# A causal convolution followed by a gated feed-forward layer: third channel group of the first chunk in bf16 on VectorE, a new order of the first loads, and a reordered VectorE list in the first step

## The chip, the cores and the metric

The kernel runs on one core of a Trainium2 chip. The metric is the device time of one execution in microseconds (us), the median of several; lower is better. TensorE is called PE below, its weight loads PEld, VectorE DVE, ScalarE ACT, GpSimd POOL, and SyncE, which issues most loads and stores, SP. A small letter q (SPq, ACTq) marks an engine's sequencer, for example when it issues a transfer.

An execution that takes over 1.5% more than the fastest of the same kernel is called slow here, the others fast. One of the kernel before took 1214.12 us and is left out.

## The reference

```python
# attention-like part: a causal convolution with one softmaxed 7-tap filter per head
w = softmax(weight, axis=-1)                 # (8 heads, 7 taps)
out[b, s, h, g] = sum_k w[h, k] * x_pad[b, s + k, h, g]    # x is (8, 4096, 192), group 24
# feed-forward part on (32768, 192)
h = x @ w_in                                 # 192 -> 2048
g = h * sigmoid(beta * h)                    # beta per feature
y = g @ w_out                                # 2048 -> 192, fp32 out
```

## The kernel before

The tokens are worked in 32 steps. A step takes 512 tokens of two sequences. The 192 channels of a token lie as three groups (c = 0, 1, 2) of 64; the two sequences fill 128 partitions. In a step PE makes 16 blocks of 128 features ("hidden"); ACT applies Silu to each block, and PE multiplies finished blocks with w_out ("output pairs"). The convolution for step s + 2 runs on DVE during step s.

Some names: a tap is one of the seven multiply-adds of the filter; cw holds the softmaxed filter weights; x0, x1 and xf are the loaded tokens of chunks 0, 1 and 2, and x0b, x1b and xb their bf16 copies; ct is the finished convolution; ph is a block of hidden features in PSUM, the memory into which PE writes, and g the block after Silu; pa and pb are PSUM tiles, of output pairs and, early in step 0, of other work. A load "lands" when its transfer is complete.

Step 0 is special, because nothing is ready for it. Its convolution is split: groups 0 and 1 on PE (products with diagonal matrices), group 2 with five taps on DVE and two on PE. Chunk 1 (the tokens of step 1) is prepared inside step 0 as well, its group 0 on PE and its groups 1 and 2 on DVE.

```python
    load_x(x0, 0)                                  # SP's queue, in this order
    nc.sync.dma_start(out=beta_q, in_=...)
    ...                                            # w_in_raw: first 256 columns, fp32, two transfers
    load_x(x1, TOK)                                # chunk 1
    for i in range(NW - 1):
        load_w_out(i)
    load(2)                                        # chunk 2
    ...
    hold = setup.tile([1, 1], BF16)                # POOL issues the other w_in columns, cast to bf16,
    nc.gpsimd.tensor_copy(hold, x0b[0:1, 0, 0, 0, 0:1])   # once the first x0 rows are cast
    load_w_in(F0, FW)
    for i in range(1, NW):
        load_w_in(i * FW, (i + 1) * FW)
    ...
    nc.scalar.copy(w_in_s[:, :, 0:F0], w_in_raw)   # ACT's list: first columns, then x1 casts and ct
    new_ct(0)
    for c in range(NG - 1):                        # groups 0 and 1: seven taps on PE
        ...
        for b in ((0, 1), (2,))[c]:
            cast_rows(nc.scalar.copy, x1b, x1, b)
        nc.scalar.copy(cts[0][:, c, :], pv[:, 0, :])
    cast_rows(nc.scalar.copy, x1b, x1, NB - 1)
    ...
    K_V = 5                                        # group 2: taps 5, 6 on PE, taps 0..4 on DVE
    pv = in_a()[:, 0, :]
    for k in range(K_V, K):
        diag_tap(k, xt0[:, NG - 1], pv, k0=K_V)
    dst = cts[0][:, NG - 1, :]
    for k in range(K_V):
        o = HALO - PAD + k
        tap(dst, xt0[:, NG - 1, o : o + TOK].bitcast(FP32), k)
    nc.vector.tensor_tensor(dst, pv, dst, ALU.add)
    ...
    first_work = {                                 # DVE's list in step 0, by block; None = next tap of chunk 1
        4: [None, lambda: scale_w_out(1), None],
        5: [None],
        6: [conv1_evac, lambda: scale_w_out(2), lambda: rows_of(2), None],
        8: [None, lambda: scale_w_out(3)],
        9: [None],
        10: [None],
    }
    QUOTA_A = {4: 2, 7: 5}                         # output pairs PE does in early blocks of step 0
```

`rows_of(2)` casts chunk 2 and starts its transposes; `scale_w_out(i)` divides a quarter of w_out by beta and casts it.

Of the kernel before, what the change touches and what calls it, by code (L numbers as in the profile page):

```python
# [9 lines left out]
FP32 = mybir.dt.float32  # L10
FP32R = mybir.dt.float32r
# [6 lines left out]
def kernel(  # L18
# [62 lines left out]
    def in_a():  # L81
        return psum_a.tile([128, 2, TOK], FP32, name="pa")
# [67 lines left out]
    w8 = setup.tile([H, K], FP32)  # L150
    nc.scalar.dma_start(out=w8, in_=weight)
    beta_q = setup.tile([NF, 128], FP32)


    def load_x(dst, t0):
        for i in range(2):
            t = t0 + i * 2 * BLK
            nc.sync.dma_start(  # L158
                out=dst[:, i].rearrange("q h b d -> q h (b d)"),
                in_=x_v[0, t : t + 2 * BLK, :, :].rearrange(  # L160
                    "(q b) h d -> q h (b d)", b=2
                ),
            )

    load_x(x0, 0)
    nc.sync.dma_start(out=beta_q, in_=moe_beta.rearrange("(c p) -> c p", p=128))
    F0 = 256
    w_in_raw = setup.tile([128, NG, F0], FP32)
    for r in range(2):
        nc.sync.dma_start(  # L170
            out=w_in_raw[r * DG : (r + 1) * DG], in_=w_in_v[:, :, 0:F0]
        )
    load_x(x1, TOK)
    for i in range(NW - 1):
        load_w_out(i)
    load(2)
# [5 lines left out]
    warm = setup.tile([H, 1], FP32)  # L182
    nc.vector.memset(warm, 0.0)  # L183
    nc.scalar.activation(warm, warm, AF.Exp)  # L184
    xt0 = setup.tile([128, NG, HALO + TOK], FP32R)
    nc.vector.memset(xt0[:, :, 0:HALO].bitcast(FP32), 0.0)

    sel = setup.tile([H, 2, DG], FP32)
    nc.gpsimd.memset(sel, 1.0)
# [38 lines left out]
    def cast_rows(copy, xb, x, b):  # L228
        copy(  # L229
            xb[:, b].rearrange("q c h p -> q h c p"),  # L230
            x[:, b // 2, :, b % 2].rearrange("q h (p c) -> q h c p", c=NG),
        )

    def transposes(pt, xb, b):
        for c in range(NG):
            nc.tensor.transpose(
                pt[:, c, :], xb[:, b, c].rearrange("q h p -> q (h p)"), ident_b
            )

    def tokens(xt, b):  # L240
        t = HALO + (b // 2) * 2 * BLK
        return xt[:, :, t : t + 2 * BLK].rearrange("p c (q b) -> p c b q", b=2)[:, :, b % 2]


    fill(3)
    pw = in_a()[:, 0, 0:K]
    nc.tensor.matmul(pw, sel.rearrange("i h p -> i (h p)"), w8, start=True, stop=True)
    fill(5)
    nmax = setup.tile([128, 1], FP32)
# [12 lines left out]
    def diags(k0, k1):  # L262
        nc.vector.tensor_tensor(
            diag[:, k0:k1],
            ident.unsqueeze(1).to_broadcast((128, k1 - k0, 128)),
            cw[:, k0:k1].unsqueeze(2).to_broadcast((128, k1 - k0, 128)),
            ALU.mult,
        )

    for b in range(NB):  # L270
        cast_rows(nc.vector.tensor_copy, x0b, x0, b)
        if b == 1:
            diags(0, 2)
    diags(2, 4)
    diags(4, K)


    hold = setup.tile([1, 1], BF16)
    nc.gpsimd.tensor_copy(hold, x0b[0:1, 0, 0, 0, 0:1])
    load_w_in(F0, FW)  # L280
    for i in range(1, NW):
        load_w_in(i * FW, (i + 1) * FW)
# [4 lines left out]
    def new_ct(s):  # L287
        cts[s] = ct_pool.tile([128, NG, TOK], BF16, name="ct")

    def diag_tap(k, xt, pv, rows=slice(0, 128), k0=0):  # L290
        o = HALO - PAD + k
        nc.tensor.matmul(  # L292
            pv,
            diag[rows, k, :],
            xt[rows, o : o + TOK],
            start=(k == k0),
            stop=(k == K - 1),
        )

# [1 line left out]
        pool.tile([128, 2, 2 * TOK], BF16, name=name)  # L301
        for pool, name in ((psum_b, "pb"), (psum_h, "ph"))
    ]
    for b in range(NB):
        pt = pts[b % 2][:, b // 2, 0 : NG * BLK].rearrange("p (c q) -> p c q", c=NG)
        transposes(pt, x0b, b)
        nc.scalar.copy(tokens(xt0, b), pt)  # L307
        if b % 2:
            fill(1, 384)
    pb = in_a()[:, 0, 0:NF]  # L310
    nc.tensor.transpose(pb, beta_q, ident[0:NF, 0:NF])
    nc.scalar.copy(beta, pb)
    fill(1, 256)
    nc.scalar.copy(w_in_s[:, :, 0:F0], w_in_raw)

    def scale_w_out(i):
        fcs = slice(i * NQ, (i + 1) * NQ)
# [9 lines left out]
    for c in range(NG - 1):  # L327
        pv = in_b() if c else psum_h.tile([128, 2, TOK], FP32, name="ph")
        for k in range(K):
            diag_tap(k, xt0[:, c], pv[:, 0, :])  # L330
        for b in ((0, 1), (2,))[c]:
            cast_rows(nc.scalar.copy, x1b, x1, b)
        nc.scalar.copy(cts[0][:, c, :], pv[:, 0, :])
    cast_rows(nc.scalar.copy, x1b, x1, NB - 1)

    def tap(dst, src, k):
        scalar = cw[:, k : k + 1]
# [4 lines left out]
                out=dst, in0=src, scalar=scalar, in1=dst, op0=ALU.mult, op1=ALU.add  # L342
            )

    K_V = 5
    pv = in_a()[:, 0, :]
    for k in range(K_V, K):
        diag_tap(k, xt0[:, NG - 1], pv, k0=K_V)
    dst = cts[0][:, NG - 1, :]
    for k in range(K_V):  # L350
        o = HALO - PAD + k
        tap(dst, xt0[:, NG - 1, o : o + TOK].bitcast(FP32), k)
    nc.vector.tensor_tensor(dst, pv, dst, ALU.add)
    nc.vector.reciprocal(beta_r, beta)
    scale_w_out(0)

# [1 line left out]
    def second():  # L358
        xt = new_xt(1)
        for i in range(2):  # L360
            pt = (in_b, in_a)[i]()
            for b in range(2):
                for c in range(NG):
                    for r in range(2):
                        rows = slice(r * DG, (r + 1) * DG)
                        o = (c * 2 + b) * DG
                        nc.tensor.matmul(
                            pt[:, r, o : o + DG],
                            x1b[rows, 2 * i + b, c].rearrange("q h p -> q (h p)"),
                            ident_b[rows, rows],  # L370
                            start=True,
                            stop=True,
                        )
            t = HALO + i * 2 * BLK
            for r in range(2):
                nc.vector.tensor_copy(
                    xt[:, :, t + r * BLK : t + (r + 1) * BLK].rearrange(
                        "p c (q b) -> p c q b", b=2
                    ),
                    pt[:, r, 0 : NG * BLK].rearrange("p (c b q) -> p c q b", c=NG, b=2),  # L380
                )
        halo(1, xt0)
        nc.vector.tensor_copy(xt1[:, HALO - PAD :], xt[:, 0, HALO - PAD :])


# [53 lines left out]
    class Job:  # L439
# [27 lines left out]
        def leave(self):  # L467
            nb = self.nb
            osb = osb_pool.tile([128, 2, D], FP32, name="osb")
            dst = osb[:, 0:nb, :].rearrange("p b d -> p (b d)")  # L470
            if nb == 1:
                nc.scalar.copy(dst, self.po[:, 0, 0:D])  # L472
            else:
                nc.vector.tensor_reduce(  # L474
                    dst,
                    self.po[:, :, 0 : nb * D].rearrange("p r n -> p n r"),
                    axis=mybir.AxisListType.X,
                    op=ALU.add,
                )
            p, c = divmod(self.s, CHUNKS)  # L480
            t = c * TOK + self.q * BLK
            nc.sync.dma_start(
                out=out_v[self.h, p, t : t + nb * BLK, :].rearrange(
                    "(b q) d -> q b d", q=BLK
                ),
                in_=osb[:, 0:nb, :],
            )
# [33 lines left out]
    def rows_of(ch):  # L521
        for h in range(2):
            cast(ch, h)
        xpose(ch)
# [2 lines left out]
    first_work = {  # L527
        4: [None, lambda: scale_w_out(1), None],
        5: [None],
        6: [conv1_evac, lambda: scale_w_out(2), lambda: rows_of(2), None],  # L530
        8: [None, lambda: scale_w_out(3)],
        9: [None],
        10: [None],
    }

    QUOTA_A = {4: 2, 7: 5}
    queue = deque()
    for s in range(N_ST):
        jobs_of(s)
        for u in range(NF):  # L540
            if s > 0 or u > 1:
                hidden(s, u)
            elif u == 0:
                phs = [hidden(0, fc, [0]) for fc in range(2)]
                for j in range(1, NG):
                    for fc in range(2):
                        hidden(0, fc, [j], phs[fc])
                second()
            if s > 0:
                output(s, u, 8 if s < N_ST - 1 else 7, "ab")  # L550
            elif u > 7:
                output(s, u, 5 if u < NF - 1 else 10, "ab")
            elif u in QUOTA_A:
                output(s, u, QUOTA_A[u], "a")
            if s == 0:
                if u in CONV1:
                    conv1(u)
                if u == min(CONV1):
                    queue.extend(conv_ops(1, 1))
                for work in first_work.get(u, []):  # L560
                    (work or queue.popleft())()
            else:
                if u % 2 and queue:
                    queue.popleft()()

                if u == 0 and s + 3 < N_CH:
                    load(s + 3)
                if u < 2 and s + 2 < N_CH:
                    cast(s + 2, u)
                if u == 1 and s + 2 < N_CH:  # L570
                    xpose(s + 2)
            if u == 12 and s + 2 < N_CH:
                queue.extend(conv_ops(s + 2, 0))
# [32 lines left out]
```

## Time and profile before

| | kernel before |
|---|---|
| first three executions | 690.76 us, 692.39 us, and the one of 1214.12 us that is left out |
| span of the profiled execution | 690.1 us |
| PE busy from 36 to 80 us | 44.00 of 44.00 us |
| first Silu; first Silu of step 1 | 13.21 us; 31.82 us |

The head of the profile page, busy time and share of the span:

```profile
span 690.1 us, 24341 instructions
PE 682.9 (99%) x11312; PEld 521.7 (76%) x11312; DVE 523.2 (76%) x466; ACT 579.8 (84%) x532; POOL 8.2 (1%) x19
```

The table by window, with the columns: stretch, its length, then busy time (and number of instructions) of PE, PEld, DVE, ACT and POOL, the granted PE clock, the DMA share and GB/s:

```profile
28.00:30.00 2.00, 2.00 (x34) 1.82 (x31) 1.97 (x3) 2.00 (x3) 0.00 (x0) 1.00 0.23 40
...
36.00:58.00 22.00, 22.00 (x374) 16.81 (x370) 18.55 (x18) 18.71 (x18) 0.00 (x0) 1.00 0.42 109
```

From 36 to 668 us the windows show no idle time of PE at all, so every microsecond that an edit of step 0 saves or costs must show in when step 1 starts.

ACT's timeline in step 0 of the kernel before. Columns: start, length, engine, line, operation, out<-in, shape, number of instructions merged; in brackets the idle time before and what ended it:

```profile
13.21 4.14 ACT L431 ACTIVATE g<-ph,beta 128x1024 bf16<-128x1024 f32 x4 [0.52 <-PE ph L423]
17.79 1.11 ACT L431 ACTIVATE g<-ph,beta 128x1024 bf16<-128x1024 f32 x1 [0.44 <-PE ph L423]
19.11 2.24 ACT L431 ACTIVATE g<-ph,beta 128x1024 bf16<-128x1024 f32 x2 [0.21 <-PE ph L423]
21.59 9.59 ACT L431 ACTIVATE g<-ph,beta 128x1024 bf16<-128x1024 f32 x9 [0.24 <-PE ph L423]
31.82 1.11 ACT L431 ACTIVATE g<-ph,beta 128x1024 bf16<-128x1024 f32 x1 [0.63 <-PE ph L423]
```

Nine Silus take 9.59 us, about 1.06 us a block. The first four Silus start 1.01 us apart, and there PE waits for ACT (the "<-ACT g" further below). From block 5 on it is PE that sets the pace: it is busy 12.00 of 12.00 us from 18 to 30 us, and each Silu starts about 0.04 us after PE's last product of its block (the ends of products are modelled). One block on PE, from the chain of waits of a second profile of this kernel (before_again; start, length, what), is 1.06 us too:

```profile
25.65 0.65 PE ph L423 x6
26.29 0.16 PE pa L456 x4
26.46 0.25 PE pb L456 x6
```

The gaps of 0.21 and 0.24 us before Silus 5 and 7 (counted from 0) lie in this stretch, in which PE is never idle: beside the blocks it works chunk 1's group 0 there. The gap of 0.44 us at 17.79 follows a wait of PE for a slice of w_in, in PE's timeline:

```profile
16.40 0.37 PE L423 MATMUL ph<-ct,w_in_s 64*128 64x512 bf16 x1 [0.20 <-ACT g L431]
16.93 0.82 PE L423 MATMUL ph<-ct,w_in_s 64*128 64x512 bf16 x5 [0.16 <-DMA w_in_s<-in_moe_w_in_dram]
```

DVE's timeline around group 2 of chunk 0 and around the casts of chunk 2:

```profile
7.86 0.49 DVE L339 TENSOR_SCALAR ct<-xt,cw 128x512 bf16<-128x512 f32 x1 [0.18 <-ACT xt L307]
8.38 3.11 DVE L341 SCALAR_TENSOR_TENSOR ct<-xt,cw,ct 128x512 bf16<-128x512 f32 x4
11.96 0.69 DVE L353 TENSOR_TENSOR ct<-pa,ct 128x512 bf16<-128x512 f32 x1 [0.46 <-PE pa L292]
...
24.46 0.69 DVE L106 CAST xb<-xf 128x768 bf16<-128x768 f32 x1 [0.56 <-DMA xf<-in_x_dram]
...
27.66 0.95 DVE L318 TENSOR_TENSOR w_out_s<-w_out_raw,beta_r 128x768 bf16<-128x768 f32 x1
28.52 2.60 DVE L341 SCALAR_TENSOR_TENSOR ct<-xt,cw,ct 128x1024 bf16<-128x1024 bf16 x2
```

And the chain of waits of this execution (start, length, what) from 8 to 32 us:

```profile
8.61 15.83 DMA xf<-in_x_dram
...
29.84 1.30 DVE ct L341
...
31.18 0.61 PE ph L423 x4
```

The reader sees two chains that end step 0 almost together: the blocks, which PE makes and ACT finishes with a Silu and which start when group 2 is ready ("the Silus" below), and DVE's list, which waits for chunk 2.

### The profile page before, as it was taken

To read this page: it belongs to the slowest core of one execution; us is meant where nothing else is said; L and a number is where in the kernel's file an instruction comes from. 1 tells how busy PE (TensorE), PEld (TensorE's weight loads), DVE (VectorE), ACT (ScalarE), POOL (GpSimd) and SP (SyncE) were. 2 spreads that over 40 slices of the span, in tenths; PEclk is the share of its full clock that TensorE was granted. 3 is DMA by queue.
4 is the path that set the end of the run, shared out by engine and by line. 5 is a ranking of instruction groups with operands and counts; after the bars stand their busy time and mean duration, and the time that the engine had idled before them with its cause. 6 is when DMAs were issued, how large, how long until landed. Compare 5 with 4: busy or idle time off the path is not lost.

```text
span 690.1 us, 24341 instructions
## 1 busy us (share of the span) xinstructions
PE 682.9 (99%) x11312; PEld 521.7 (76%) x11312; DVE 523.2 (76%) x466; ACT 579.8 (84%) x532; POOL 8.2 (1%) x19
## 2 busy tenths in 40 slices
PE   8999999999999999999999999999999999999997
PEld 4877777777777777777777777777777777777776
DVE  6888877788777797777797777887777977777721
ACT  7888888888888888888888888888888888888883
POOL 4000000000000000000000000000000000000000
PEclk9999999999999999999999999999999999999999
DMA  9744332244332343332444332443322443322111
GB/s 234 175 110 116 105 94 77 75 116 116 94 102 65 91 116 107 100 101 56 103 117 105 94 90 62 116 116 96 103 70 83 117 114 89 104 54 59 48 36 59
DMA packets 121861, 67.06 MB, mean 97 GB/s; under 512 B 53264, under 2 KB 121760, under 8 KB 121760
## 3 DMA queue, kind: packets, MB, share of 16 engines
q1 hardware_dynamic: 120080, 64.13, 34.4%
q0 software_dynamic: 1664, 1.38, 1.2%
q8 instruction: 88, 1.44, 0.9%
q14 instruction: 13, 0.11, 0.1%
q10 hardware_dynamic: 16, 0.00, 0.0%
HBM read 29.89 MB, written 25.17 MB: 80 GB/s over the span
## 4 chain that ended last, share of the span: by engine, by line
PE 95%; DMA 3%; DVE 1%; SPq 0%; ACT 0%; issue 0%
PE ph L423 47%; PE pa L456 24%; PE pb L456 24%; DMA xf<-in_x_dram 2%; DVE ct L341 1%; DMA x<-in_x_dram 1%; SPq L95 0%; ACT g L431 0%; SPq L148 0%; DVE w_out_s L318 0%; DVE xb L106 0%; SPq L158 0%; ACT osb L472 0%; DVE xt L121 0%
## 5 line engine op out<-in xcount | busy, mean ns | idle before, releaser
L431 ACT ACTIVATE g<-ph,beta 128x1024 bf16<-128x1024 f32 x512 | 569.6, 1114 | 96.6 <-PE ph L423 90.7
L456 PEld LDWEIGHTS <-g 64*128 64x128 bf16 x8160 | 371.2, 94 | 102.5 <-ACT g L431 0.7
L423 PE MATMUL ph<-ct,w_in_s 64*128 64x512 bf16 x3072 | 425.6, 376 | 1.3 <-ACT g L431 1.1
L341 DVE SCALAR_TENSOR_TENSOR ct<-xt,cw,ct 128x1536 bf16<-128x1536 bf16 (+2 forms) x190 | 337.6, 1777 | 2.5
L456 PE MATMUL pa<-w_out_s,g 64*128 64x192 bf16 x4112 | 246.6, 243 | 0.5 <-ACT g L431 0.5
L456 PE MATMUL pb<-w_out_s,g 64*128 64x192 bf16 (+1 forms) x4048 | 230.9, 243 | 0.0
L423 PEld LDWEIGHTS <-w_in_s 64*128 64x128 bf16 x3072 | 160.2, 94 | 55.4 <-DMA w_in_s<-in_moe_w_in_dram 1.8
L474 DVE TENSOR_REDUCE osb<-pa 128x384 f32<-128x768 f32 x64 | 61.3, 957 | 125.3 <-PE pa L456 125.2
L474 DVE TENSOR_REDUCE osb<-pb 128x384 f32<-128x768 f32 x63 | 60.5, 960 | 26.8 <-PE pb L456 26.8
L106 DVE CAST xb<-xf 128x768 bf16<-128x768 f32 x60 | 41.2, 686 | 0.6 <-DMA xf<-in_x_dram 0.6
L339 DVE TENSOR_SCALAR ct<-xt,cw 128x1536 bf16<-128x1536 bf16 (+2 forms) x32 | 31.2, 974 | 0.2 <-ACT xt L307 0.2
L472 ACT COPY osb<-pb 128x192 f32<-128x192 f32 x1 | 0.3, 318 | 6.5 <-PE pb L456 6.5
L226 PE MATMUL ph<-zeros 128*128 128x512 bf16 (+2 forms) x11 | 4.4, 513 | 1.1 <-DVE warm L183 1.1
L214 POOL DMA_DIRECT2D w_in_s<-in_moe_w_in_dram x8 | 5.1, 647 | 0.0
L292 PE MATMUL pb<-xt,diag 64*128 64x512 f32 (+1 forms) x21 | 5.0, 434 | 0.0
L121 DVE COPY xt<-xt 128x18 bf16<-128x18 bf16 x27 | 4.7, 175 | 0.0
L292 PEld LDWEIGHTS pb<-xt,diag 64*128 64x128 f32 (+1 forms) x21 | 3.1, 187 | 0.7
L318 DVE TENSOR_TENSOR w_out_s<-w_out_raw,beta_r 128x768 bf16<-128x768 f32 x3 | 2.9, 954 | 0.0
L226 PEld LDWEIGHTS <-zeros 128*128 128x128 bf16 x11 | 1.2, 121 | 2.2 <-issue 1.1
L229 ACT CAST x1b<-x 128x384 bf16<-128x384 f32 x4 | 2.7, 708 | 0.0
L184 ACT ACT_TABLE_LOAD x1 | 1.3, 1283 | 1.4 <-PEq L590 1.4
L229 DVE CAST x0b<-x 128x384 bf16<-128x384 f32 x4 | 1.6, 434 | 0.9 <-DMA x<-in_x_dram 0.9
(53 smaller groups left out, 26.3 us busy)
## 6 DMA issues: line engine op xcount, KB each, us to landing
out_dram<-osb SPq DMA_DIRECT2D x127, 192.0 KB, 2.2
xf<-in_x_dram SPq DMA_DIRECT2D x60, 384.0 KB, 4.2
xt<-xb SPq DMA_TRANSPOSE x120, 2.5
x<-in_x_dram SPq DMA_DIRECT2D x4, 384.0 KB, 5.0
w_out_raw<-in_moe_w_out_dram SPq DMA_DIRECT2D x4, 384.0 KB, 12.8
w_in_s<-in_moe_w_in_dram POOLq DMA_DIRECT2D x6, 192.0 KB, 10.7
w_in_raw<-in_moe_w_in_dram SPq DMA_DIRECT2D x2, 192.0 KB, 5.0
w_in_s<-in_moe_w_in_dram POOLq DMA_DIRECT2D x2, 96.0 KB, 7.5
```

The costliest lines, as they stand in the source:

```text
L106: nc.vector.tensor_copy(xbs[ch][:, :, :, h, :], xfs[ch][:, h].rearrange("q b (p c) -> q b c p", c=NG),)
L121: nc.vector.tensor_copy(dst, last[:, :, HALO + TOK - PAD :])
L214: nc.gpsimd.dma_start(out=w_in_s[r * DG : (r + 1) * DG, :, c0:c1], in_=w_in_v[:, :, c0:c1])
L226: nc.tensor.matmul(pf[:, 0, 0:cols], zeros, zc, start=True, stop=True)
L229: copy(xb[:, b].rearrange("q c h p -> q h c p"), x[:, b // 2, :, b % 2].rearrange("q h (p c) -> q h c p", c=NG),)
L292: nc.tensor.matmul(pv, diag[rows, k, :], xt[rows, o : o + TOK], start=(k == k0), stop=(k == K - 1),)
L339: nc.vector.tensor_scalar_mul(dst, src, scalar)
L341: nc.vector.scalar_tensor_tensor(out=dst, in0=src, scalar=scalar, in1=dst, op0=ALU.mult, op1=ALU.add)
L423: nc.tensor.matmul(ph[:, h, :], w_in_s[rows, j, fc * 128 : (fc + 1) * 128], cts[s][rows, j, :], start=(j == 0), stop=(j == NG - 1),)
L431: nc.scalar.activation(gs[s][:, fc], ph, AF.Silu, scale=beta[:, fc : fc + 1])
L456: nc.tensor.matmul(self.po[:, r, b * D : (b + 1) * D], g[rows, fc, self.h, q * BLK : (q + 1) * BLK], w_out_s[rows, fc, :], start=(self.don ...
L474: nc.vector.tensor_reduce(dst, self.po[:, :, 0 : nb * D].rearrange("p r n -> p n r"), axis=mybir.AxisListType.X, op=ALU.add,)
```

## The change

Its intent: let DVE read group 2 as bf16 and finish it without PE; bring chunk 1 in before the first w_in columns; release the other w_in slices as soon as cw exists; and put DVE's list in the order in which the loads land, so that two taps come ahead of the wait for chunk 2. ACT's list changes with it: the cast of the first w_in columns moves behind the first copy of ct. Cut to its core:

```diff
+    nc.scalar.dma_start(out=beta_q, in_=...)              # was on SP's queue, after x0
     load_x(x0, 0)
+    load_x(x1, TOK)                                       # was after w_in_raw
...
-    nc.gpsimd.tensor_copy(hold, x0b[0:1, 0, 0, 0, 0:1])
+    nc.gpsimd.tensor_copy(hold, cw[0:1, 0:1])
...                                                        # third transposes go to pt_v, DVE copies them out
+        nc.vector.tensor_copy(
+            xt0_v[:, t : t + 2 * BLK].rearrange("p (q b) -> p b q", b=2), pt_v[:, i]
+        )
...
-    nc.scalar.copy(w_in_s[:, :, 0:F0], w_in_raw)
...
+        if c == 0:
+            for b in range(2):
+                cast_rows(nc.scalar.copy, x1b, x1, b)
         nc.scalar.copy(cts[0][:, c, :], pv[:, 0, :])
+        if c == 0:
+            nc.scalar.copy(w_in_s[:, :, 0:F0], w_in_raw)
...
-    K_V = 5                                               # two taps on PE, five on DVE, one add
...
+    for k in range(K):                                    # all seven on DVE
+        tap(cts[0][:, NG - 1, :], xt0_v[:, o : o + TOK], k)
+    cast_rows(nc.vector.tensor_copy, x1b, x1, 3)          # was on ACT
...
-            nc.sync.dma_start(
+            (nc.scalar if nb == 1 else nc.sync).dma_start(   # the last two stores
...
-        6: [conv1_evac, lambda: scale_w_out(2), lambda: rows_of(2), None],
-        8: [None, lambda: scale_w_out(3)],
-        9: [None],
-        10: [None],
+        6: [conv1_evac, lambda: scale_w_out(2), None],
+        7: [None, lambda: rows_of(2)],
+        8: [None, lambda: scale_w_out(3)],
+        9: [None],
...
-    QUOTA_A = {4: 2, 7: 5}
+    QUOTA_A = {4: 2, 7: 4, 8: 4}                          # two pairs fewer in step 0
```

More of the change, by code (lines that the diff above doesn't have):

```diff
@@ L152 @@
     beta_q = setup.tile([NF, 128], FP32)
+    nc.scalar.dma_start(out=beta_q, in_=moe_beta.rearrange("(c p) -> c p", p=128))
     def load_x(dst, t0):
@@ L165 @@
     load_x(x0, 0)
-    nc.sync.dma_start(out=beta_q, in_=moe_beta.rearrange("(c p) -> c p", p=128))
+    load_x(x1, TOK)
     F0 = 256
@@ L172 @@
         )
-    load_x(x1, TOK)
     for i in range(NW - 1):
@@ L184 @@
     nc.scalar.activation(warm, warm, AF.Exp)
-    xt0 = setup.tile([128, NG, HALO + TOK], FP32R)
+    xt0 = setup.tile([128, NG - 1, HALO + TOK], FP32R)
+    xt0_v = setup.tile([128, HALO + TOK], BF16)
     nc.vector.memset(xt0[:, :, 0:HALO].bitcast(FP32), 0.0)
+    nc.vector.memset(xt0_v[:, 0:HALO], 0.0)
     sel = setup.tile([H, 2, DG], FP32)
@@ L232, in cast_rows, with transpose @@
         )
-    def transposes(pt, xb, b):
-        for c in range(NG):
-            nc.tensor.transpose(
-                pt[:, c, :], xb[:, b, c].rearrange("q h p -> q (h p)"), ident_b
-            )
+    def transpose(dst, xb, b, c):
+        nc.tensor.transpose(dst, xb[:, b, c].rearrange("q h p -> q (h p)"), ident_b)
     def tokens(xt, b):
@@ L245 @@
     fill(3)
-    pw = in_a()[:, 0, 0:K]
+    pc = in_a()
+    pw = pc[:, 0, 0:K]
+    pt_v = pc[:, 1, 0 : TOK // 2].bitcast(BF16).rearrange("p (i b q) -> p i b q", i=2, b=2)
     nc.tensor.matmul(pw, sel.rearrange("i h p -> i (h p)"), w8, start=True, stop=True)
@@ L268, in diags @@
         )
-    for b in range(NB):
-        cast_rows(nc.vector.tensor_copy, x0b, x0, b)
-        if b == 1:
-            diags(0, 2)
-    diags(2, 4)
-    diags(4, K)
-    hold = setup.tile([1, 1], BF16)
-    nc.gpsimd.tensor_copy(hold, x0b[0:1, 0, 0, 0, 0:1])
+    hold = setup.tile([1, 1], FP32)
+    nc.gpsimd.tensor_copy(hold, cw[0:1, 0:1])
     load_w_in(F0, FW)
@@ L288, in new_ct, with diag_tap @@
         cts[s] = ct_pool.tile([128, NG, TOK], BF16, name="ct")
-    def diag_tap(k, xt, pv, rows=slice(0, 128), k0=0):
+    def diag_tap(k, xt, pv, rows=slice(0, 128)):
         o = HALO - PAD + k
@@ L295, in diag_tap @@
             xt[rows, o : o + TOK],
-            start=(k == k0),
+            start=(k == 0),
             stop=(k == K - 1),
@@ L303 @@
     ]
-    for b in range(NB):
-        pt = pts[b % 2][:, b // 2, 0 : NG * BLK].rearrange("p (c q) -> p c q", c=NG)
-        transposes(pt, x0b, b)
-        nc.scalar.copy(tokens(xt0, b), pt)
-        if b % 2:
-            fill(1, 384)
-    pb = in_a()[:, 0, 0:NF]
-    nc.tensor.transpose(pb, beta_q, ident[0:NF, 0:NF])
-    nc.scalar.copy(beta, pb)
-    fill(1, 256)
-    nc.scalar.copy(w_in_s[:, :, 0:F0], w_in_raw)
+    for i in range(2):
+        for b in (2 * i, 2 * i + 1):
+            cast_rows(nc.vector.tensor_copy, x0b, x0, b)
+            pt = pts[b % 2][:, i, 0 : 2 * BLK].rearrange("p (c q) -> p c q", c=NG - 1)
+            for c in range(NG - 1):
+                transpose(pt[:, c, :], x0b, b, c)
+            nc.scalar.copy(tokens(xt0, b), pt)
+            transpose(pt_v[:, i, b % 2, :], x0b, b, NG - 1)
+        if i == 0:
+            fill(1, 384)
+            diags(0, 2)
+        else:
+            fill(1, 384)
+            pb = pts[0][:, 1, TOK : TOK + 2 * NF].bitcast(FP32)
+            nc.tensor.transpose(pb, beta_q, ident[0:NF, 0:NF])
+            nc.scalar.copy(beta, pb)
+            fill(1, 256)
+    for i in range(2):
+        if i == 1:
+            diags(2, 4)
+            diags(4, K)
+        t = HALO + i * 2 * BLK
+        nc.vector.tensor_copy(
+            xt0_v[:, t : t + 2 * BLK].rearrange("p (q b) -> p b q", b=2), pt_v[:, i]
+        )
     def scale_w_out(i):
@@ L330 @@
             diag_tap(k, xt0[:, c], pv[:, 0, :])
-        for b in ((0, 1), (2,))[c]:
-            cast_rows(nc.scalar.copy, x1b, x1, b)
+        if c == 0:
+            for b in range(2):
+                cast_rows(nc.scalar.copy, x1b, x1, b)
         nc.scalar.copy(cts[0][:, c, :], pv[:, 0, :])
-    cast_rows(nc.scalar.copy, x1b, x1, NB - 1)
+        if c == 0:
+            nc.scalar.copy(w_in_s[:, :, 0:F0], w_in_raw)
+    cast_rows(nc.scalar.copy, x1b, x1, 2)
     def tap(dst, src, k):
@@ L343, in tap @@
             )
-    K_V = 5
-    pv = in_a()[:, 0, :]
-    for k in range(K_V, K):
-        diag_tap(k, xt0[:, NG - 1], pv, k0=K_V)
-    dst = cts[0][:, NG - 1, :]
-    for k in range(K_V):
+    for k in range(K):
         o = HALO - PAD + k
-        tap(dst, xt0[:, NG - 1, o : o + TOK].bitcast(FP32), k)
-    nc.vector.tensor_tensor(dst, pv, dst, ALU.add)
+        tap(cts[0][:, NG - 1, :], xt0_v[:, o : o + TOK], k)
+    cast_rows(nc.vector.tensor_copy, x1b, x1, 3)
     nc.vector.reciprocal(beta_r, beta)
@@ L381, in second @@
                 )
-        halo(1, xt0)
+        dst = xt[:, :, HALO - PAD : HALO]
+        nc.vector.tensor_copy(dst[:, 0 : NG - 1], xt0[:, :, HALO + TOK - PAD :])
+        nc.vector.tensor_copy(dst[:, NG - 1], xt0_v[:, HALO + TOK - PAD :])
         nc.vector.tensor_copy(xt1[:, HALO - PAD :], xt[:, 0, HALO - PAD :])
@@ L550 @@
                 output(s, u, 8 if s < N_ST - 1 else 7, "ab")
-            elif u > 7:
+            elif u > 8:
                 output(s, u, 5 if u < NF - 1 else 10, "ab")
```

## The prediction

> **What bounds the kernel.** TensorE, after the first 31 us. In the table by window PE is busy 22.00 of 22.00 us from 36 to 58 us and from 58 to 80; one step is 16 x 1.31 = 21.0 us, and 32 are 671 of the 690.1 us. The change touches step 0 and the last 3 us only, so its ceiling is about 19 us (estimate: 690.1 - 671).
>
> Within step 0 (timeline, 0 to 36 us):
> - The first w_in matmuls start at 11.85; they wait for group 2 of ct until the add ends at 12.65; the first Silu starts at 13.21.
> - From there ScalarE paces the step: 16 Silus at 1.065 us (9 took 9.59), plus gaps of 0.44 + 0.21 + 0.24 us, the first after PE's wait for a w_in slice (landed 16.93). Last end: 31.18.
> - VectorE ends chunk 1's taps at 31.13; PE starts step 1 at 31.18 after 0.46 us of idle. The chain of waits runs through those taps and the chunk 2 load, which VectorE awaits until 24.46.
>
> So two chains, ScalarE's and VectorE's, end step 0 together.
>
> **Costs.**
> 1. Group 2: two fp32 tap matmuls (PE 0.63 us) and the 0.69 us add go; two more taps at 0.78 us come (3.11/4; I expect no gain from bf16: taps cost 1.30 us at 1024 elements, 1.78 at 1536), plus two VectorE evacuations from PSUM (0.35 us each, estimate from 0.50 for 384 elements) and one x1 cast (0.42). The first tap falls from 0.49 to about 0.33. VectorE starts tapping at about 8.45 instead of 7.86 and ends at 13.4 instead of 12.65. PE reaches the w_in matmuls at 11.3 but waits for group 2: first Silu at 13.9 to 14.0, 0.75 us later.
> 2. DMA order: x1 goes ahead of w_in_raw, beta leaves its queue; w_in slices are released by cw (about 4.2) rather than the x0 cast (5.04), 0.9 us earlier. The Trainium skill, "DMA: Bandwidth & Descriptors" (Issuing engines are not separate DMA queues), says all queues share the same 16 engines; the trace agrees: from 11 to 20 us both queues are active and the total stays near 236 GB/s. Bytes are reordered, not saved. The w_in wait at 16.9 should vanish (0.4 to 0.9 us on ScalarE's chain). w_in_raw lands near 10 instead of 8.2, just in time for its cast, now after the first ct evacuation.
> 3. VectorE's list: two taps move ahead of the chunk 2 casts, filling its waits of 0.56 and 1.12 us; but it starts about 1.1 us late. End of chunk 1's taps: again about 31.1. Two output pairs (0.16 us) move to later steps.
> 4. Last two stores from ScalarE's queue: at most 0.1 us.
>
> **Sum.** Silu chain: 14.0 + 16 x 1.065 = 31.05 against 31.18; VectorE 31.1 against 31.13; +0.16 for pairs, -0.1 at the end, and a risk of 0.4 us that w_out's last scaling (29.8 instead of 28.6) stalls PE at feature block 14. Net -0.8 to +0.7 us, inside the spread of executions (690.76, 692.39). I predict 691.7 us, 690.2 to 693.4 in 8 of 10. Chances: faster by over 2% 0.005, within 2% 0.99, slower 0.005.
>
> **What would show it.** Windows from 36 us on unchanged; 128x512 bf16 taps at 0.75 to 0.82 us each, after a first of 0.33; first Silu at 13.9; no w_in wait at 16.9; VectorE not waiting for the chunk 2 load; step 1 starting between 30.6 and 31.7.
>
> **What would make it wrong.** w_in_raw landing after 11 us; x0's second half delayed by the earlier w_in transfers; bf16 taps much faster than 0.78 us (up to 1 us gain); VectorE's later list stalling PE in blocks 12 to 15.

## The result

The changed kernel took 692.36 us (median of four, 692.25 to 692.53). The three fast runs of the kernel before of that occasion were 690.76, 692.39 and 693.47, and the ratio is 1.0002 with a 95% interval of 0.9978 to 1.0027. A ratio here is the mean time of one kernel's fast runs over that of the other's fast runs of the same rounds, so it is not quite the ratio of the medians that are quoted. A repetition on one chip with more rounds (the run after_again below) gave 692.52 against 691.36 us, ratio 1.0019, interval 1.0007 to 1.0032: the change costs about 0.2% (0.5 to 2.2 us by the interval).

The span of the profiled execution is 690.5 us. The table by window after:

```profile
28.00:30.00 2.00, 1.68 (x29) 1.10 (x26) 2.00 (x3) 2.00 (x3) 0.00 (x0) 1.00 0.25 49
...
36.00:58.00 22.00, 22.00 (x376) 16.88 (x372) 18.56 (x16) 18.86 (x17) 0.00 (x0) 1.00 0.43 110
```

From 36 us on PE is as busy as before. A hole is new: PE was busy 2.00 of 2.00 us between 28 and 30 us before, and is busy 1.68 now. ACT's timeline after:

```profile
13.91 5.17 ACT L440 ACTIVATE g<-ph,beta 128x1024 bf16<-128x1024 f32 x5 [1.02 <-PE ph L432]
19.29 2.24 ACT L440 ACTIVATE g<-ph,beta 128x1024 bf16<-128x1024 f32 x2 [0.21 <-PE ph L432]
21.79 8.44 ACT L440 ACTIVATE g<-ph,beta 128x1024 bf16<-128x1024 f32 x8 [0.25 <-PE ph L432]
30.67 1.12 ACT L440 ACTIVATE g<-ph,beta 128x1024 bf16<-128x1024 f32 x1 [0.44 <-PE ph L432]
32.14 1.11 ACT L440 ACTIVATE g<-ph,beta 128x1024 bf16<-128x1024 f32 x1 [0.36 <-PE ph L432]
```

The first Silu is 0.70 us later than before. The gap at 17.79 us is gone, and a new one of 0.44 us stands before the last Silu of the step. PE's timeline tells why the new gap is there, and what the first w_in products wait for:

```profile
11.85 1.09 PE L432 MATMUL ph<-ct,w_in_s 64*128 64x512 bf16 x8 [1.01 <-ACT w_in_s L345]
13.42 0.61 PE L432 MATMUL ph<-ct,w_in_s 64*128 64x512 bf16 x4 [0.48 <-DVE ct L353]
...
29.39 0.34 PE L465 MATMUL pa<-w_out_s,g 64*128 64x192 bf16 x4 [0.32 <-DVE w_out_s L327]
```

DVE's timeline after, the same two places:

```profile
6.67 0.45 DVE L321 COPY xt_v<-pa 128x256 bf16<-128x256 bf16 x1 [0.61 <-PE pa L238]
...
7.81 0.45 DVE L321 COPY xt_v<-pa 128x256 bf16<-128x256 bf16 x1
8.29 0.35 DVE L351 TENSOR_SCALAR ct<-xt_v,cw 128x512 bf16<-128x512 bf16 x1
8.68 4.69 DVE L353 SCALAR_TENSOR_TENSOR ct<-xt_v,cw,ct 128x512 bf16<-128x512 bf16 x6
...
25.93 1.27 DVE L106 CAST xb<-xf 128x768 bf16<-128x768 f32 x2
...
28.39 0.95 DVE L327 TENSOR_TENSOR w_out_s<-w_out_raw,beta_r 128x768 bf16<-128x768 f32 x1
29.25 1.28 DVE L353 SCALAR_TENSOR_TENSOR ct<-xt,cw,ct 128x1024 bf16<-128x1024 bf16 x1
```

DVE no longer waits for chunk 2. But the last quarter of w_out is scaled at 29.34 (28.39 + 0.95) instead of 28.61 us, and PE needs it from 29.1 us on. The chain of waits now runs through DVE's list into that product:

```profile
28.47 0.88 DVE w_out_s L327
...
29.39 0.34 PE pa L465 x4
```

### The profile page after: what moved, and what is told of

Read it like the earlier page. It is cut to its first block, busy times and chain, and to the rows that moved or that the text cites. A ratio compares the mean times of both kernels' runs of the same rounds, so it can differ in the third digit from the quotient of the medians.

```text
span 690.5 us, 24341 instructions
## 1 busy us (share of the span) xinstructions
PE 682.6 (99%) x11310; PEld 520.0 (75%) x11310; DVE 525.2 (76%) x472; ACT 579.1 (84%) x531; POOL 8.3 (1%) x19
## 4 chain that ended last, share of the span: by engine, by line
PE 97%; DVE 2%; ACT 1%; issue 0%; ACTq 0%
PE ph L432 47%; PE pa L465 24%; PE pb L465 24%; DVE ct L353 1%; ACT g L440 1%; PE ph L229 1%; DVE w_out_s L327 0%; PE pb L287 0%; DVE ct L411 0%; DVE xb L106 0%; DVE xt_v L321 0%; DVE diag L265 0%; PE pa L249 0%; PE ph L238 0%; PE pb L238 0%
## 5 line engine op out<-in xcount | busy, mean ns | idle before, releaser
L353 DVE SCALAR_TENSOR_TENSOR ct<-xt,cw,ct 128x1536 bf16<-128x1536 bf16 (+1 forms) x186 | 334.0, 1796 | 2.3
L351 DVE TENSOR_SCALAR ct<-xt,cw 128x1536 bf16<-128x1536 bf16 (+1 forms) x31 | 30.7, 989 | 0.0
L353 DVE SCALAR_TENSOR_TENSOR ct<-xt_v,cw,ct 128x512 bf16<-128x512 bf16 x6 | 4.5, 752 | 0.2
```

The source lines that it names most:

```text
L351: nc.vector.tensor_scalar_mul(dst, src, scalar)
L353: nc.vector.scalar_tensor_tensor(out=dst, in0=src, scalar=scalar, in1=dst, op0=ALU.mult, op1=ALU.add)
```

## The experiments

The change has separable parts, named A (group 2 in bf16 on DVE, with ACT's new list), B (the order of the loads and the release of w_in) and C (DVE's list in step 0, the quotas of pairs, the last two stores). The theory after the result: step 0 ends with the later of the Silus and DVE's list; A starts the Silus late, C makes PE wait for w_out, and B gives back less than that. The rivals: the loads bind step 0 as a whole, so A is hidden; or the wait for chunk 2, which C takes away, was what held step 1.

All twelve runs were correct and had five rounds. A little arithmetic ties them together: in the profiles, span minus the first Silu of step 1 is 658.3 us for the kernel before (690.12 - 31.82) and 658.4 for the changed one (690.55 - 32.14). The same difference is 658.2 to 658.6 us in every other profile but that of b_only (659.05 us; it is about 0.75 us longer than the others between its last copy and the end of the span). So, b_only apart, the first Silu of step 1 tells a profiled execution's time, free of anything later. Times before are 691.45, 691.36 and 691.64 us in the first, second and third call.

| run | parts | median us | ratio to before, 95% interval | first Silu | fifth minus first | last end minus ninth start | step 1's first Silu |
|---|---|---|---|---|---|---|---|
| first profile of before | | 692.39 | | 13.21 | 4.58 | 8.53 | 31.82 |
| before_again | | 691.53 | 0.9998 (0.9985 to 1.0010) | 13.17 | 4.05 | 8.53 | 31.12 |
| after_again | A B C | 692.52 | 1.0019 (1.0007 to 1.0032) | 13.91 | 4.05 | 8.98 | 32.13 |
| a_only | A | 692.16 | 1.0010 (0.9996 to 1.0023) | 14.02 | 4.05 | 8.53 | 32.03 |
| b_only | B, old ACT list | 693.84 | 1.0033 (1.0020 to 1.0045) | 15.06 | 4.05 | 8.53 | 32.87 |
| bc | B C, old ACT list | 694.23 | 1.0037 (1.0024 to 1.0049) | 15.27 | 4.69 | 8.98 | 34.13 |
| scale_first | A B C, w_out earlier | 692.02 | 1.0006 (0.9993 to 1.0019) | 14.19 | 4.05 | 8.49 | 31.91 |
| c_only | C | 692.07 | 1.0008 (0.9996 to 1.0021) | 13.26 | 4.64 | 8.98 | 32.06 |
| bc_act | B C, new ACT list, old group 2 | 691.76 | 1.0013 (0.9999 to 1.0027) | 13.20 | 4.05 | 8.99 | 31.43 |
| bc_act_scale | the same, w_out earlier | 691.33 | 0.9994 (0.9981 to 1.0008) | 13.43 | 4.36 | 8.49 | 31.47 |
| c_scale | C, w_out earlier | 691.44 | 0.9996 (0.9984 to 1.0009) | 13.30 | 4.43 | 8.49 | 31.40 |
| mix | see below | 691.01 | 0.9996 (0.9983 to 1.0008) | 13.04 | 4.06 | 8.45 | 30.89 |
| mix_again | the same | 691.02 | 0.9993 (0.9981 to 1.0006) | 12.84 | 4.06 | 8.46 | 30.78 |

"Fifth minus first" (starts of Silus of step 0) is 4.05 us when PE finds its w_in slice landed, and longer when ACT had a gap there (in bc the gap has another cause, see there); "last end minus ninth start" is about 8.5 us when PE does not wait for w_out and 9.0 when it does.

By the times alone only after_again, b_only and bc differ clearly from the kernel before; the other intervals hold 1. What single parts are worth is therefore read from the profiles, one or two executions each.

### Part A alone

```diff
 # the kernel before, with A only: xt0_v, its two copies out of PSUM, seven taps on DVE,
 # ACT's new list, chunk 1's last cast on DVE
-    K_V = 5
+    for k in range(K): tap(cts[0][:, NG - 1, :], xt0_v[:, o : o + TOK], k)
```

> The kernel before with group 2 of chunk 0 in bf16 by VectorE alone, and nothing else of the change. My theory (step 0 ends with the later of ScalarE's Silu chain and VectorE's list; the late group 2 costs): first Silu at 13.9 to 14.2 us against 13.21, the w_in wait near 16.9 gone because PE comes later, VectorE still waiting for or close behind the chunk 2 load; step 1 starts 0.2 to 0.6 us later than in the kernel before and the time is 0.2 to 0.6 us longer. Rival (step 0 is bound by its loads, so group 2 is hidden): first Silu later all the same, but step 1 starts and the time ends within 0.1 us of the kernel before.

Measured: first Silu at 14.02 us, step 1's first Silu at 32.03, 692.16 us against 691.45. The time rose by 0.7 us, slightly more than the theory's range, and step 1's first Silu came 0.21 us later than in the first profile of the kernel before and 0.91 later than in the second; the rival "within 0.1 us" falls in the medians, though the interval of the ratio (0.9996 to 1.0023) by itself would not exclude it. The run bc_act below decides the point.

### Parts B, and B with C, with ACT's old list

```diff
 # b_only: the kernel before with B only; bc: with B and C
+    nc.scalar.dma_start(out=beta_q, in_=...)
     load_x(x0, 0)
+    load_x(x1, TOK)                       # ahead of w_in_raw
-    nc.gpsimd.tensor_copy(hold, x0b[0:1, 0, 0, 0, 0:1])
+    nc.gpsimd.tensor_copy(hold, cw[0:1, 0:1])
```

> The kernel before with only the order of the loads changed (beta from ScalarE's queue, chunk 1 ahead of the first w_in columns, the other w_in slices released by cw). My theory: first Silu at 12.9 to 13.2, its gap near 17 us smaller, but VectorE still waits for chunk 2 until about 24.4 and ends chunk 1's taps at about 31.1, so the time is within 0.2 us of the kernel before. Rival (loads bind step 0): step 1 starts 0.5 us or more earlier and the time falls by as much.

> The change with group 2 put back as it was (five fp32 taps on VectorE, two on PE, one add), so the order of the loads and VectorE's list remain. My theory: first Silu at 12.9 to 13.2, VectorE does not wait for the chunk 2 load, step 1 starts at 30.2 to 30.9 and the time is 0.4 to 0.9 us below the kernel before and below the changed kernel: group 2 eats what the rest gains. Rival (group 2 is neutral, the change as a whole has nothing to give): within 0.2 us of the changed kernel.

Both expectations missed, mainly by the same oversight of mine: 693.84 and 694.23 us, 2.4 and 2.8 us above the kernel before instead of equal and below. ACT's timeline of b_only shows it:

```profile
10.47 0.83 ACT L314 CAST w_in_s<-w_in_raw 128x768 bf16<-128x768 f32 x1 [2.79 <-DMA w_in_raw<-in_moe_w_in_dram]
11.21 1.31 ACT L229 CAST x1b<-x 128x384 bf16<-128x384 f32 x2
```

With chunk 1 ahead of it, w_in_raw lands at 10.4 us instead of 8.2. ACT works its list in order, the cast of w_in_raw stood at its head, and so chunk 1's casts and the copies of ct waited 2.79 us behind it; the first Silu came at 15.06. The old list and the new order of loads do not go together. I had cut the change at the wrong joint: ACT's list belongs to B, not to A. Neither run says anything about group 2.

Two more things lie in these numbers. Of b_only's 2.4 us, about 0.75 lie after its last copy in the profile, and no run here shows why. And in the profiled execution of bc the granted PE clock fell to 0.50 for 3.4 us from 15.0 us on. The window of step 0 shows it as a mean of 0.95 (the third number from the right), where no other profile is below 1.00:

```profile
0.00:36.00 36.00, 31.37 (x322) 19.22 (x324) 25.12 (x45) 28.07 (x36) 8.14 (x19) 0.95 0.79 192
```

The gap behind bc's 4.69 us is from this stretch and not from a w_in slice (the fourth landed at 16.54 us, before it was needed). The two executions of bc at full clock took 693.24 and 693.32 us, the three at 0.998 took 694.23 to 695.12: about 1.8 us of the 2.8 are left for the edit.

### Group 2 put back, ACT's new list kept

```diff
 # bc_act: the changed kernel with the old arithmetic of group 2 (and, with it, the old transposes of chunk 0)
+    K_V = 5
+    for k in range(K_V, K): diag_tap(k, xt0[:, NG - 1], pv, k0=K_V)
+    for k in range(K_V): tap(dst, xt0[:, NG - 1, o : o + TOK].bitcast(FP32), k)
     cast_rows(nc.vector.tensor_copy, x1b, x1, 3)
+    nc.vector.tensor_tensor(dst, pv, dst, ALU.add)
```

> The changed kernel with only the arithmetic of group 2 put back (five fp32 taps on VectorE, two on PE, one add), and ScalarE's new list kept: the run named bc had put ScalarE's old list back too, which waits for w_in_raw at its head. My theory: first Silu at 12.8 to 13.2 instead of 13.9, but the fourth w_in slice still lands at about 16.9 (its landing was 16.9 in both kernels) and holds block 4, so of the 0.9 us only about 0.3 reach the step's end: time 0.1 to 0.5 us below the changed kernel. Rival (group 2 is the whole loss): 0.7 us or more below the changed kernel. Third possibility (group 2 costs nothing): within 0.1 us.

> The changed kernel itself, so that the others of this call have it on the same chip. Both theories: 0.3 to 0.9 us above the kernel before in the same rounds; step 1's first Silu at about 32.1 us.

Measured in the same rounds: 691.76 us against 692.52 for the changed kernel, 0.76 us less in the medians and 0.57 in the means (692.15 against 692.71); the five times of each overlap (691.64 to 693.12 and 692.12 to 693.76), so the times alone do not settle it. ACT's timeline of bc_act shows where the difference lies:

```profile
13.20 5.17 ACT L434 ACTIVATE g<-ph,beta 128x1024 bf16<-128x1024 f32 x5 [0.45 <-PE ph L426]
...
31.43 1.11 ACT L434 ACTIVATE g<-ph,beta 128x1024 bf16<-128x1024 f32 x1 [0.36 <-PE ph L426]
```

First Silu 13.20 against 13.91 (0.71 earlier), step 1's first Silu 31.43 against 32.13 (0.70 earlier). The first of these repeats: the four profiles with group 2 on DVE alone have their first Silu at 13.91 to 14.19 us, the eight with the old group 2 (b_only and bc apart, which the late w_in_raw holds) at 12.84 to 13.43. The second rests on one profile of each: in these two executions the lateness of group 2 reaches the end of the step in full. My theory's reservation, that a late w_in slice would eat most of it, did not come true in this one: the slice landed at 16.05 us, before it was needed. In bc_act_scale below, with the same loads, it landed at 16.89 and cost 0.31 us. The rival's size, 0.7 us, fits the profiles; its words "the whole loss" do not, since bc_act is still 0.40 us above the kernel before in the medians and 0.76 in the means. The changed kernel's own repetition came out somewhat worse than expected (1.16 us above the kernel before, expected 0.3 to 0.9).

### The last scaling of w_out ahead of its tap

```diff
 # scale_first: the changed kernel
-        8: [None, lambda: scale_w_out(3)],
+        8: [lambda: scale_w_out(3), None],
```

> The changed kernel with two entries of VectorE's list swapped: the last scaling of w_out ahead of a tap in block 8. My theory: the wait of PE for w_out_s at 29.4 us and the Silu gap of 0.44 us after it go, the last Silu of step 0 ends about 0.4 us earlier and the time falls 0.3 to 0.5 us below the changed kernel. Rival (VectorE's chunk 1 taps would have held step 1 anyway): they end at about 30.5 either way, step 1 moves by less than 0.1 us.

The gap before the last Silu is gone; ACT's timeline:

```profile
14.19 5.17 ACT L440 ACTIVATE g<-ph,beta 128x1024 bf16<-128x1024 f32 x5 [1.42 <-PE ph L432]
...
22.05 9.50 ACT L440 ACTIVATE g<-ph,beta 128x1024 bf16<-128x1024 f32 x9 [0.24 <-PE ph L432]
31.91 1.11 ACT L440 ACTIVATE g<-ph,beta 128x1024 bf16<-128x1024 f32 x1 [0.36 <-PE ph L432]
```

From the ninth Silu's start to the last one's end it took 8.49 us, against 8.98 in the changed kernel: 0.49 us saved. The first Silu happened to be 0.28 us later in this execution, so step 1's first Silu moved by only 0.23. By the ratios to before (1.0006 against 1.0019) the gain is near 0.9 us, but these come from different chips. The wait in block 14 is shown as the cause of the 0.44 us gap; the rival (DVE's taps would have held step 1 anyway) falls, since step 1 followed the last Silu by 0.36 us as in the changed kernel, although DVE's taps ended later (30.92 us instead of 30.54).

### Part C alone, and with the earlier scaling

```diff
 # c_only: the kernel before with C; c_scale: also
-        8: [None, lambda: scale_w_out(3)],
+        8: [lambda: scale_w_out(3), None],
```

> The kernel before with only VectorE's list and the quotas of the first step changed, and the last two stores from ScalarE's queue. My theory: VectorE no longer waits for chunk 2 and ends chunk 1's taps before 30.9, but the last scaling of w_out comes about 0.8 us later than in the kernel before and holds PE in block 14 as in the changed kernel (Silus 8 to 15 take 9.0 us instead of 8.5), so the time is within 0.4 us of the kernel before. Rival (the wait for chunk 2 was what held step 1): time falls by 0.5 us or more.

> The run c_only with the last scaling of w_out ahead of its tap: the kernel before with its own loads, own group 2 and own ScalarE list. Theory: step 1's first Silu falls from 32.06 to about 31.55 and the time 0.4 to 0.6 us below c_only, 0 to 0.4 us below the kernel before. If it equals bc_act_scale within 0.1 us, the new order of the loads is worth nothing; if it stays 0.3 us or more above, the order of the loads is worth that.

c_only: 692.07 us, 0.7 us above the kernel before in the medians (mean 691.94 against 691.38; the interval of the ratio holds 1) where I had allowed 0.4. DVE ended chunk 1's taps at 30.46 us, as expected, and the Silus 8 to 15 took 8.98 us, as expected. The run does not test the rival cleanly, because it takes away the wait for chunk 2 and brings in the wait for w_out of 0.45 us at once; c_scale has the first without the second. c_scale: 691.44 us, step 1's first Silu at 31.40; the last Silus took 8.49 us. That is 0.2 us below the kernel before of its rounds (0.34 in the means), as expected, but not clear of noise. c_only ran in another call; by the ratios to before (1.0008 and 0.9996) c_scale is about 0.8 us lower, and by step 1's first Silu 0.66. The rival's 0.5 us or more is not borne out: from the last Silu of step 0 to the first of step 1 it is 0.36 us in both runs, against 0.63 and 0.50 in the two profiles of the kernel before, so DVE's list, with its wait for chunk 2, had held step 1 by 0.27 and 0.14 us.

The comparison of c_scale with bc_act_scale judges the order of the loads, since the two differ in B and ACT's list alone:

```diff
 # bc_act_scale: bc_act and
-        8: [None, lambda: scale_w_out(3)],
+        8: [lambda: scale_w_out(3), None],
```

> The run bc_act with the last scaling of w_out ahead of its tap, and without the other two edits of mix. Theory: the wait in block 14 was all that mix gained over bc_act, so step 1's first Silu is at 30.8 to 31.1 and the time within 0.2 us of mix. Rival (the split slice and the earlier w_in_raw of mix carry part of it): 31.2 or later, and 0.3 us or more above mix.

Measured: 691.33 us (mean of five 691.27) against 691.44 for c_scale (mean 691.31), step 1's first Silu at 31.47 and 31.40. The new order of the loads, together with the ACT list that it needs, shows no gain here; with five executions each, one of 0.3 us could hide in the noise. Against mix the theory misses: step 1's first Silu was at 31.47 where I expected 30.8 to 31.1, and the time lies 0.31 us above mix_again (0.16 in the means). This profiled execution waited for its w_in slice (fifth minus first is 4.36 us), which mix's split slice avoids, so the rival has the better of it; with 0.3 us between medians and one profile each it is not settled.

### A second profile of the kernel before

> The kernel before itself, for a second profile of it: its first profiled execution took 691.87 us where its median on this chip is 691.4. If landings and waits are the same, step 1's first Silu is again at 31.6 to 31.9 us; if that first profile was a slow execution, it is at 31.2 to 31.5, and the readings that use 31.82 have to be corrected by the difference. Ratio to itself within 0.05% of 1.

This is the run that corrected most. ACT's timeline in the second profile:

```profile
13.17 5.17 ACT L431 ACTIVATE g<-ph,beta 128x1024 bf16<-128x1024 f32 x5 [0.51 <-PE ph L423]
...
31.12 1.11 ACT L431 ACTIVATE g<-ph,beta 128x1024 bf16<-128x1024 f32 x1 [0.50 <-PE ph L423]
```

The gap of 0.44 us at 17.79 us, which I had read as a cost of the kernel, is not there. The fourth w_in transfer, which block 4 needs, landed at 16.08 us in this execution and at 16.89 in the first. That is not the chip: c_only has the same loads in the same order, ran on the chip of this second profile, and there the transfer landed at 17.00 us, with the gap back (0.49 us). Step 1's first Silu came at 31.12, outside the range expected for a repetition and even before that for a slow first profile. The first profile (691.87 us) was of an execution slower than this one (691.14 us). Neither is the odd one out: the 32 executions of the kernel before in the three calls lie between 690.87 and 692.96 us with a median of 691.49, nine of them at or below 691.14 and three above 691.87. Nor is the gap rare: of the four profiled executions with these loads and this group 2, three have it (0.44 us here, 0.49 in c_only, 0.28 in c_scale). So all readings that use 31.82 have to be taken against 31.12 as well.

### A version of the parts that pay

```diff
 # mix: bc_act_scale, and
-    load_x(x1, TOK)
+    load_x(x1, TOK, [0])                  # first half, then w_in_raw, then the second half
...
+    load_x(x1, TOK, [1])
...
-    for i in range(1, NW):
+    for c0 in (FW, FW + F0):              # the second w_in slice in two pieces of 256 columns
+        load_w_in(c0, c0 + F0)
+    for i in range(2, NW):
```

> The run bc_act with three more edits: the first w_in columns between the two halves of chunk 1, the second w_in slice in two pieces of 256 columns, and the last scaling of w_out ahead of its tap. My theory: w_in_raw lands near 9.0, first Silu at 12.4 to 12.8, block 4 is not held (its piece lands near 15.4), no w_out wait in block 14; step 1's first Silu at 30.4 to 31.2 and the time 0.6 to 1.4 us below the kernel before. Rival (the loads bind step 0 in total): step 1's first Silu stays at 31.6 to 32.1.

> The run mix once more, to settle it against the kernel before with ten executions in place of five: 0.2 to 0.6 us below it, about 0.05%, and step 1's first Silu at 30.7 to 31.1.

Measured: 691.01 and 691.02 us; step 1's first Silu at 30.89 and 30.78. ACT's timeline of mix:

```profile
13.04 5.17 ACT L437 ACTIVATE g<-ph,beta 128x1024 bf16<-128x1024 f32 x5 [0.52 <-PE ph L429]
...
30.89 1.11 ACT L437 ACTIVATE g<-ph,beta 128x1024 bf16<-128x1024 f32 x1 [0.36 <-PE ph L429]
```

It is 1.5 us (0.2%) below the changed kernel of the same rounds, and the five times of each do not overlap. The piece of w_in for block 4 landed at 15.22 us (second half, fourth transfer), and PE did not wait for it in either profile. The first Silu came later than expected (12.4 to 12.8 expected), as the second half of w_in_raw landed at 10.0 (mix) and 9.5 us (mix_again), not near 9.0. Against the kernel before both runs are lower, by 0.35 and 0.62 us in the medians, where I had expected 0.6 to 1.4 for mix (missed) and 0.2 to 0.6 for mix_again; but both intervals hold 1: that mix beats the kernel before is likely and not shown.

## Why the prediction was right, and where its steps failed

The time (692.36 us) lies in the predicted range of 690.2 to 693.4, and "within 2%" was right. It was right because the reach of the change was read correctly from the windows (nothing between 36 and 668 us moved) and because the range of 3.2 us was wide. Inside that reach the sum was too kind: "Net -0.8 to +0.7 us" with a centre slightly below the kernel before, where the repetition showed 1.16 us above it. That the time fell inside the range all the same is owed to the width of the range.

Between two profiles the span can be written as a sum of what each stretch gave. Against the first profile of the kernel before it rose by 0.43 us (690.55 - 690.12), against the second by 1.12 us (690.55 - 689.43):

| stretch | first profile of before | before_again | after | difference to the first | to before_again |
|---|---|---|---|---|---|
| first Silu | 13.21 | 13.17 | 13.91 | +0.70 | +0.74 |
| first to ninth Silu | 9.45 | 8.92 | 8.89 | -0.56 | -0.03 |
| ninth Silu to the last one's end | 8.53 | 8.53 | 8.98 | +0.45 | +0.45 |
| from there to step 1's first Silu | 0.63 | 0.50 | 0.36 | -0.27 | -0.14 |
| from there to the end | 658.30 | 658.31 | 658.41 | +0.11 | +0.10 |

The sum itself had a slip. "Silu chain: 14.0 + 16 x 1.065 = 31.05" leaves out the gaps of 0.21 and 0.24 us, which the kernel before has inside its 31.18 and which stayed (0.21 and 0.25 us after). The last Silu ended at 31.78 us, 0.73 later than that sum: these two gaps, the 0.44 us of w_out, and 0.17 us the other way.

Point by point:

1. *Group 2.* "First Silu at 13.9 to 14.0, 0.75 us later": 13.91. Its parts were nearly right too. The taps took 752 ns each with bf16 input and 752 ns with fp32 input (the groups of both profiles; the 1.78 us that the prediction gives for 1536 elements is 1.82 in the trace); the first tap fell from 486 to 354 ns (predicted 0.33 us). The copies out of PSUM were sized at 0.35 us and took 0.446. The Trainium skill, "VectorE: DVE Perf Modes" (The perf-mode tier table), gives bf16 a gain for tensor_scalar over fp32, and says that a PSUM operand caps the mode; the 486 to 354 ns agree with the first. The 446 ns of a copy of only 256 elements would fit the second, but these copies also write every other element, and no run here tells the two apart. It does not list the fused multiply-add of the other six taps, and that one did not gain. So the bf16 input sped up one instruction by 0.13 us, and two more taps and two copies came.
2. *The w_in wait.* "The w_in wait at 16.9 should vanish (0.4 to 0.9 us on ScalarE's chain)": the wait did vanish, but not for the reason given, and not as a gain to count on. The reason given was that the slices are issued 0.9 us earlier. POOL issued the first slice at 4.28 instead of 5.30 us, and the fourth landed at 16.87 instead of 16.89 (second profiles: 16.32 and 16.08). Over all profiles with the old order of loads it landed at 16.08 to 17.00 us (five, mean 16.64), with the new one at 16.05 to 16.89 (seven, mean 16.54; mix, whose slices are cut differently, is left out). The wait was gone because PE came 0.7 us later. Against the first profile the vanished wait gives back 0.56 of the 0.70 us by which group 2 was late, within the 0.4 to 0.9 us predicted; against the second, which has no such wait, it gives nothing. I had subtracted from a single execution what only some executions have. Why the earlier issue brought hardly any earlier landing is open; two things are on record. The first is the DMA view of 11 to 20 us, before and then after (queue and kind: packets, MB, share of the 16 engines):

```profile
q0 software_dynamic: 1318, 1.11, 74.9%
q1 hardware_dynamic: 1326, 0.99, 43.7%
```

```profile
q0 software_dynamic: 1305, 1.11, 75.0%
q1 hardware_dynamic: 1363, 1.02, 44.4%
```

   POOL's queue (software_dynamic) moves 1.11 MB in that stretch in both kernels, while SP's queue (hardware_dynamic) moves about 1 MB. The packets of the two queues are nearly equal in number, as the Trainium skill, "DMA: Bandwidth & Descriptors" (Queues, rings and completion order), has it: each DMA engine takes turns between its queues, packet by packet. So neither queue gained on the other in that stretch. The second is that POOL's queue moved nothing at all until 9.87 us in the kernel before and 9.75 in the changed one: its first packet came 4.5 to 5.5 us after its first issue in every profile here, while SP's queue was moving data (1.25 MB from 5.3 to 9.8 us before). What POOL's queue waited for in that time was not tested; taking turns does not explain it.
3. *DVE's list.* "End of chunk 1's taps: again about 31.1": it ended at 30.54 us, because the taps moved ahead filled the waits even better than costed. This took away the 0.14 to 0.27 us by which DVE had held step 1, and no more, because the Silus ended last from then on.
4. *w_out.* The stall that the prediction named "a risk of 0.4 us" is a certainty: 0.45 us in the table, 0.44 in ACT's gap, all five profiles with this list have it (after, after_again, bc, bc_act, c_only: 8.98 to 8.99 us), and three runs that only move the scaling ahead of a tap (scale_first, c_scale, bc_act_scale) lose it. It should have stood in the sum as a cost. The prediction had its time nearly right (29.8 us against a measured 29.34).
5. *Small terms.* Two pairs fewer in step 0 add 0.16 us at the end (from the last Silu's end to the last copy's start: 7.80 us before, 7.96 after). That the last stores from ACT's queue give something back is not shown: from the last copy's start to the end of the span it is 3.41 us before and 3.36 after, but 3.50 in after_again and 3.31 in a_only, which has the old stores (predicted: 0.1 us at most).
6. *w_in_raw.* "Lands near 10, just in time for its cast": it landed at 10.88 us, the cast waited 1.14 us for it, and PE 1.01 us for the cast. This was hidden, because group 2 was later still (13.4 us).
7. *The pace.* "From there ScalarE paces the step" holds for the first four or five Silus only. From block 5 on PE has no idle time and its work sets the 1.06 us a block (see the profile before). The number was right by luck, since the two engines are within 0.05 us of each other; the reason matters, because a stall of PE in these blocks, as that for w_out, cannot be hidden.

In one sentence: DVE's wait for chunk 2, which had held step 1 by 0.14 to 0.27 us, was traded for PE's wait of 0.45 us for w_out from the same list, and the two taps of group 2 that PE had worked in 0.63 us were moved to DVE, whose part of group 2 then ended at 13.37 instead of 12.65 us and held the first Silu.

## What to carry to other kernels

A wait that one profile shows behind a load may be the scatter of that execution's landings: take more profiles before counting its removal as a gain. When a list of one engine is reordered to fill a wait, ask of each item that moves back who needs it and when. Moving work to the engine whose result the others wait for delays them all: here group 2 became ready 0.7 us later, and in the one pair of profiles that isolates it (bc_act and after_again) all of it reached the end of the step. And when a sum of terms is compared with a measured time, put every gap of the measured chain into the sum, or say why it goes.

## What the Trainium skill lacked or had wrong

- "VectorE: DVE Perf Modes" (The perf-mode tier table) has no row for the fused multiply-add with a per-partition scalar and a tensor (SCALAR_TENSOR_TENSOR in the trace). It took 752 ns for 128x512 with bf16 and with fp32 input alike, and 1282 ns for 128x1024 in bf16: no gain from 16-bit operands.
- "DMA: Bandwidth & Descriptors" (Latency and other measured facts) gives no figure for scatter. The same transfer of the same kernel landed at 16.89 us in one execution and 16.08 us in another, with other queues busy (17.00 us in c_only and 16.83 in c_scale, which have the same loads), and PE's wait for it was there in three of these four and absent in one.
- The same page's formula for one transfer (Anatomy of one DMA: about 2.0 us plus the bytes at 436 GB/s) gives 2.2 to 2.5 us for the w_in slices of 96 to 192 KB (an estimate from the page). In the kernel before they landed 7.4 to 13.9 us after their issue: the formula does not cover transfers that are issued one behind the other into a busy stretch, and the page gives no figure for these.
